# A planner's GpSimd price corrected, and a limit on how far a background step may push attention's scores back

## The chip, the cores and the metric

The kernel runs on one core of a Trainium2 chip. The metric is the time of one execution on the device, in microseconds. The profiled execution is a run of its own with its own time.

## The reference

One conformer block over x of shape (2, 4000, 144), bfloat16, with four heads of 36 and a depthwise convolution of five taps. `_layernorm` has no weights.

```python
h = _layernorm(x); x = x + 0.5 * (_silu(h @ w_ff1a) @ w_ff1b)
h = _layernorm(x); q, k, v = split(h @ w_qkv)          # each (B, H, T, 36)
p = _softmax(q @ k.T * 36 ** -0.5)                      # over 4000 keys
x = x + (p @ v) @ w_o
h = _layernorm(x) @ w_pw1; h = h[..., :144] * _sigmoid(h[..., 144:])
c = sum(pad(h)[:, i:i + T] * dw[i] for i in range(5))   # along time
x = x + _silu(c) @ w_pw2
h = _layernorm(x); x = x + 0.5 * (_silu(h @ w_ff2a) @ w_ff2b)
return _layernorm(x)
```

## The kernel before

**Tiling.** A batch has 4000 tokens in eight chunks: seven of 512 and a last one of 416. Chunks 0 to 7 are batch 0, 8 to 15 batch 1. Within a chunk, a token tile holds 128 tokens (104 in the last chunk), and most steps handle half a chunk, two tiles, at a time (index g).

**Attention.** A group is (batch, query chunk, pair of heads p), 32 groups in all. Within a group an iteration handles 128 keys: `emit_S` issues four score matmuls into two PSUM banks, `emit_exp` one exp on ScalarE over both banks (1024 columns, 832 in the last chunk), `emit_O` four value matmuls into banks 4 and 5. 4000 keys are 31 such iterations and a remainder of 32, which is handled for both pairs together in an iteration of its own in the group with p = 0 (tile PR). Two sets of banks alternate, so the scores of iteration n wait for the exp of n - 2. When the last values of a group are issued, `epilogue` copies banks 4 and 5 out on VectorE (OTA, OTF), transposes OTF on TensorE and divides by the sums (AN). The next group's first values may only be issued when OTF is done.

**Background.** All other work of a chunk is a background step: `ff1` and `pre2` (first feed-forward, then keys, queries and values) ahead of its attention, `post1` (output projection, residual, gate `glu`) and `post2` (convolution `conv`, second feed-forward, last layer norm, store) behind it. The convolution of chunk c waits for `glu` of chunk c + 1, unless c is its batch's last. During attention, gates use tanh on ScalarE (tile TH), which shares its function table with exp, and only banks 6 and 7 are open to background steps. Two series of `post2` run beside each other, for even and odd chunks.

**Layer norm.** `ln` takes statistics on VectorE (`bn_stats`, `bn_aggr`), adds epsilon and raises to -0.5 on GpSimd (tile RS), and normalises two tiles (XN). In the middle of attention (`rest`) the normalise is always on GpSimd. Before all keys of batch 0 are there, and after the last exp, it takes GpSimd or VectorE, by a comparison of planned times. `transp` then transposes XN on TensorE.

**The order.** All engines run their queues in order, and a planner in Python writes the order out. `Rec.op` keeps a planned time for each engine: an instruction starts when its engine is free and its operands are done, lasts `cost`, and is done `LAT` later; on TensorE a change of `kind` adds 0.13. Every background step is a generator (`Thread`) that yields the engine it needs next. `Sched.best` takes, among the threads in list order, the first whose start lies within 0.15 of the earliest. The main loop compares that start t with a, the time at which the next scores can start:

```python
a = s_start(n_s) if n_s < NIT else R.free["pe"]
t, th = S.best()
if th is not None and (a is None or t < a or (th.req[0] == "act" and t < a + 0.05)):
    S.run(th)
```

So a background step goes ahead of the next scores if it starts before them, however long it is. `a` is None while the keys of the next scores' chunk are not there. The planned costs of TensorE steps are 0.24 for a half's transposes or projection, 0.43 for a feed-forward, gate or projection tile, 0.60 for the ten matmuls of a feed-forward's second product, 0.84 for the epilogue's transposes and 1.07 for one half of a convolution.

Every instruction is recorded through one line, so the profile gives all of them line L135; tiles tell them apart.

Of the kernel before, what the change touches and what calls it, by code (L numbers as in the profile page):

```python
# [145 lines left out]
class Slots:  # L146
# [11 lines left out]
    def best(self):  # L158
        return min(self.free.values())
# [11 lines left out]
class Thread:  # L171
    def __init__(self, gen, ready):
        self.gen, self.ready, self.live = gen, ready, True
        self.req = ("none", None, (), None)


def need(eng, slots=None, kids=(), cond=None):
    return (eng, slots, kids, cond)


class Sched:
# [38 lines left out]
            th.ready = max(th.ready, max(o.done for o in new))  # L220

    def start_of(self, th):
        eng, slots, kids, cond = th.req
        if any(k.live for k in kids) or (cond is not None and not cond()):
            return None
        t = max([th.ready] + [k.ready for k in kids])
        if slots is not None:
            if not slots.free:
                return None
            t = max(t, slots.best())  # L230
        return max(t, self.R.free[eng]) if eng in self.R.free else t

    def best(self, window=0.15):
        c = [(self.start_of(th), th) for th in self.threads]
        c = [(t, th) for t, th in c if t is not None]
        if not c:
            return None, None
        lim = min(t for t, _ in c) + window
        return next((t, th) for t, th in c if t <= lim)

    def run(self, th):
        eng, slots, kids, cond = th.req
        for k in kids:
            th.ready = max(th.ready, k.ready)
        self.advance(th, slots.take() if slots is not None else None)


def bass_standalone__conformer_family_zipformer__speech_kernel(
# [31 lines left out]
    R = Rec(nc)  # L280
    op = R.op
    S = Sched(R)
# [4 lines left out]
    NXN, NXT, NTH, NHT, NSW = 8, 6, 6, 3, 2  # L287
    NPT = 6
    NU = 5
    NWARM = 36  # L290
    X = sb("X", [NBLK, D])
    XN = sb("XN", [NXN, 2, D])
    ST = sb("ST", [NXN, 2, 6], F32)
    MV = sb("MV", [NXN, 2, 2], F32)
# [4 lines left out]
    HT = sb("HT", [NHT, 9, CH // 2])  # L299
# [108 lines left out]
    banks = Slots(R, range(8))  # L408
# [14 lines left out]
            op("dve", "tensor_copy", dst, src, r=r, w=w, cost=dve)  # L423

    def setup_dw():
        bk = yield need("pe", banks)
        for k in range(2):
            op("pe", "transpose", PSH[0:HD, bk, k * 8:k * 8 + KCONV], DWR[0:KCONV, k * HD:(k + 1) * HD],
               IDENT[0:KCONV, 0:KCONV], r=["DWR", "ID"], w=[("ps", bk)], kind="s")
        yield need("dve")  # L430
        op("dve", "tensor_scalar", DWT[0:HD, :, 0:KCONV],
           PSH[0:HD, bk, 0:16].rearrange("p (k n) -> p k n", k=2)[:, :, 0:KCONV], 0.5, None, op0=ALU.mult,
           r=[("ps", bk)], w=["DWT"])
        banks.give(bk)
# [13 lines left out]
    def transp(c, src, rk, s, g):  # L448

        n = tb(c)  # L450
        bk = yield need("pe", banks)
        dst = PSH[0:HD, bk, 0:512].rearrange("p (k i n) -> p k i n", k=2, i=2)
        for k in range(2):
            for i in range(2):
                op("pe", "transpose", dst[:, k, i, 0:n], src[:, i, k * HD:(k + 1) * HD], IDENT[0:n, 0:n],
                   r=rk + ["ID"], w=[("ps", bk)], cost=0.06, kind="f")
        yield need("dve")
        xd = XT[0:HD, s, :, g * 2 * n:(g + 1) * 2 * n].rearrange("p k (i n) -> p k i n", i=2)
        copy(xd, dst[:, :, :, 0:n], [("ps", bk)], [("XT", s, g)], 0.37, 0.48)
        banks.give(bk)  # L460

    def ln(c, g):
        n = tb(c)
        u = yield need("dve", xnp)
        for i in range(2):
            op("dve", "bn_stats", ST[0:n, u, i, :], X[0:n, c * NB + 2 * g + i, :], r=[("X", c, 2 * g + i)],
               w=[("ST", u, i)], cost=0.233)
        yield need("dve")
        for i in range(2):
            op("dve", "bn_aggr", MV[0:n, u, i, :], ST[0:n, u, i, :], r=[("ST", u, i)], w=[("MV", u)], cost=0.09)  # L470
        op("pool", "tensor_scalar", RS[0:n, u, :, 1], MV[0:n, u, :, 1], LN_EPS, None, op0=ALU.add,
           r=[("MV", u)], w=[("VE", u)], cost=0.25)
        op("pool", "tensor_tensor", RS[0:n, u, :, 0], RS[0:n, u, :, 1], NHALF[0:n, :], op=ALU.pow,
           r=[("VE", u), "NHALF"], w=[("RS", u)], cost=0.6)
        rest = not (mode["front"] or mode["tail"])
        yield need("pool" if rest else "dve")
        for i in range(2):
            ready = R.last
            e = "dve"
            if rest or max(R.free["pool"], ready) + 0.5 < max(R.free["dve"], ready) + 0.25:  # L480
                e = "pool"
            op(e, "tensor_scalar", XN[0:n, u, i, :], X[0:n, c * NB + 2 * g + i, :], MV[0:n, u, i, 0:1],
               RS[0:n, u, i, 0:1], op0=ALU.subtract, op1=ALU.mult, r=[("X", c, 2 * g + i), ("MV", u), ("RS", u)],
               w=[("XN", u, i)], cost=0.25 if e == "dve" else 0.56)
        return u

    def ln_tr(c, s, g):
# [1 line left out]
        yield from transp(c, XN[0:tb(c), u, :, :], [("XN", u, 0), ("XN", u, 1)], s, g)  # L489
        xnp.give(u)  # L490

    def residual(c, g, mm, scale, rk, cost=0.06):

        bk = yield need("pe", banks)
        for i in (2 * g, 2 * g + 1):
            terms = mm(i)
            for t, (l, rh) in enumerate(terms):
                op("pe", "matmul", PSV[0:tb(c), bk, (i % 2) * D:(i % 2 + 1) * D], lhsT=l, rhs=rh, start=t == 0,
                   stop=t == len(terms) - 1, r=rk, w=[("ps", bk)], cost=cost, kind="f")
        yield need("dve")  # L500
        op("dve", "scalar_tensor_tensor", out=xv(c, g), in0=PSV[0:tb(c), bk, 0:2 * D].rearrange("p (i d) -> p i d", i=2),
           scalar=scale, in1=xv(c, g), op0=ALU.mult, op1=ALU.add, r=[("ps", bk)] + xk(c, g), w=xk(c, g), cost=0.46)
        banks.give(bk)
# [20 lines left out]

    def ff_tile(c, s, h, m, WA, nm, silu):

        bk = yield need("pe", banks)
        n = nc_(c)
        wk = [(nm, "a", j) for j in range(4)]
        if m < 4:  # L530
# [20 lines left out]
    def ff(c, s, WA, WB, nm, silu, then):  # L551

        h = yield need("pe", htp)
        n = tb(c)
        kids = S.spawn(ff_tile(c, s, h, m, WA, nm, silu) for m in range(5))
        yield need("pe", kids=kids)
        xtp.give(s)

        def half(g):
            yield from residual(  # L560
                c, g,
                lambda i: [(ht(h, m, CH)[:, i * n:(i + 1) * n], WB[:, m, :]) for m in range(4)]
                + [(ht(h, 4, CH // 2)[:, i % 2 * n:(i % 2 + 1) * n], WB[:, 4 + i // 2, :])],
                0.5 if silu else 0.25, [("HT", h)] + [(nm, "b", j) for j in range(5)])
            yield from then(g)

        kids = S.spawn(half(g) for g in range(2))
        yield need("pe", kids=kids)
        htp.give(h)

    def proj(Tt, Wt, nm, c, s, p):
        n = nc_(c)
        bk = yield need("pe", banks)
        for k in range(2):
            op("pe", "matmul", PSV[:, bk, 0:n], lhsT=Wt[0:HD, k, 2 * p:2 * p + 2, :].rearrange("p h d -> p (h d)"),
               rhs=XT[0:HD, s, k, 0:n], start=k == 0, stop=k == 1, r=[("XT", s, 0), ("XT", s, 1), nm], w=[("ps", bk)],
# [5 lines left out]
    def vproj(c, s, g):  # L582

        tiles = [j for j in (2 * g, 2 * g + 1) if (j + 1) * KTL <= nc_(c)]
        bk = yield need("pe", banks)
        for j in tiles:
            for k in range(2):
                op("pe", "matmul", PSV[:, bk, (j % 2) * D:(j % 2 + 1) * D], lhsT=XT[0:HD, s, k, j * KTL:(j + 1) * KTL],
# [9 lines left out]
    def vrem(c, s):  # L598

        b = c // CPB  # L600
        r0 = nc_(c) - REM
        bk = yield need("pe", banks)
        for h in range(H):
            for k in range(2):
                op("pe", "matmul", PSV[32 * h:32 * h + 32, bk, 0:DH], lhsT=XT[0:HD, s, k, r0:r0 + REM],
# [47 lines left out]

    def glu(c, s, hf):
        cc = c % CPB
        bk = yield need("pe", banks)
        n, nt = nc_(c), tb(c)
        mm2(c, WP1, s, D + hf * HD, D + (hf + 1) * HD, bk, HD, ["WP1"])
        t = yield from tanh(n, bk, HD)
        banks.give(bk)  # L660
        bk = yield need("pe", banks)
        mm2(c, WP1, s, hf * HD, (hf + 1) * HD, bk, HD, ["WP1"])
        yield need("dve")
        op("dve", "scalar_tensor_tensor", out=U[0:HD, c % NU, hf, :, 1:1 + nt],
# [37 lines left out]

    def conv(c, z, hf, silu):
        v, n, nt = c % NU, nc_(c), tb(c)
        bk = yield need("pe", banks)
        o = PSV[0:HD, bk, 0:n].rearrange("p (i n) -> p i n", i=NB)
        u = U[0:HD, c % NU, hf, :, :]
        parts = [(2, 0, 4, 0, 1), (1, 1, 4, 0, 1), (1, 0, 1, 3, 0), (0, 2, 4, 0, 1), (0, 0, 2, 2, 0),
# [52 lines left out]
    def epilogue(b, qc, p, gi):  # L761
# [2 lines left out]
        op("dve", "tensor_copy", OTA[:, 0:n], PSV[:, 4, 0:n], r=[("ps", 4)], w=["OTA"], cost=0.63)  # L764
        op("dve", "tensor_tensor", OTF[:, gi % 2, 0:n], PSV[:, 5, 0:n], OTA[:, 0:n], op=ALU.add,
           r=[("ps", 5), "OTA"], w=[("OTF", gi % 2)], cost=0.63)
        bk = yield need("pe", banks)
        for i in range(NB):
            op("pe", "transpose", PSV[0:nt, bk, i * 128:(i + 1) * 128], OTF[:, gi % 2, i * nt:(i + 1) * nt],
               IDF[:, :], r=[("OTF", gi % 2), "IDF"], w=[("ps", bk)], cost=0.21, kind="f")  # L770
        if p == 0:
            an_of[c] = yield need("dve", anp)
        a = an_of[c]
        yield need("dve")
        v = PSV[0:nt, bk, :].rearrange("p (i h d) -> p i h d", i=NB, h=2)
        op("dve", "reciprocal", RD[0:nt, gi % 2, :, :], v[:, :, :, DH], r=[("ps", bk)], w=[("RD", gi % 2)],
           cost=0.14)
# [108 lines left out]

    while n_e < NIT:
        a = s_start(n_s) if n_s < NIT else R.free["pe"]
        t, th = S.best()
        if th is not None and (a is None or t < a or (th.req[0] == "act" and t < a + 0.05)):  # L890
            S.run(th)
            if mode["front"] and len(kv_done) == CPB:
# [56 lines left out]
```

## Time and profile before

| | us |
|---|---|
| median of 3 runs | 1149.72 (1145.28 to 1159.77) |
| profiled execution | 1162.85 |
| its span, first to last instruction | 1161.0 |
| ScalarE busy | 1043.6 (90%) |
| TensorE busy | 963.1 (83%), granted clock 0.962 of full on average |
| VectorE, GpSimd busy | 467.4 (40%), 354.3 (31%) |

The profile is of one execution, and its time stands above the runs of the table's first line. In the rows, PE is TensorE, PEld its weight loads, ACT ScalarE, DVE VectorE and POOL GpSimd. A bracket at a row's end is the idle time of that engine just before it, with what ended it.

### The profile page before, as it was taken

How to read it: one execution, taken by the hardware profiler on the slowest of the kernel's cores; microseconds unless marked ns; L12 is line 12 of the kernel's file. 1: busy time of each engine (PE TensorE's matmuls, PEld its weight loads, DVE VectorE, ACT ScalarE, POOL GpSimd, SP SyncE). 2: the span in 40 equal slices, each digit the busy share in tenths (PEclk: the TensorE clock that was granted, in tenths of full speed). 3: DMA queues.
4: the chain of work that ended last, by engine and by line, in shares of the span. 5: the costliest groups of instructions: out<-in, count | busy, mean ns of one | idle time of the engine just before them, and what ended most of it. 6: DMA issues, size and time to landing. Idle time of an engine off the chain costs nothing.

```text
span 1161.0 us, 25201 instructions
## 1 busy us (share of the span) xinstructions
PE 963.1 (83%) x10834; PEld 368.7 (32%) x10834; DVE 467.4 (40%) x1445; ACT 1043.6 (90%) x1274; POOL 354.3 (31%) x595
## 2 busy tenths in 40 slices
PE   8998887999989887787879887787878787887966
PEld 4633232333333332232323221232322232222324
DVE  6875443565555543241332430241323232242424
ACT  3789999999999999999997999999999999999952
POOL 3421423354545433122232330122213123132122
PEclk8999999999999999999996899999999999999976
DMA  4000000000000000000000000000000000000000
GB/s 114 2 1 1 2 1 1 1 2 5 4 7 1 1 7 6 1 1 6 2 7 1 6 5 1 1 1 6 2 6 1 6 1 6 1 4 5 1 6 10
DMA packets 9496, 7.22 MB, mean 6 GB/s; under 512 B 2808, under 2 KB 9384, under 8 KB 9384
## 3 DMA queue, kind: packets, MB, share of 16 engines
q1 hardware_dynamic: 8228, 5.13, 1.5%
q8 instruction: 85, 1.39, 0.5%
q10 hardware_dynamic: 1156, 0.47, 0.2%
q14 instruction: 27, 0.22, 0.1%
HBM read 3.30 MB, written 2.30 MB: 5 GB/s over the span
## 4 chain that ended last, share of the span: by engine, by line
ACT 40%; PE 33%; POOL 16%; DVE 7%; issue 2%; DMA 0%; ACTq 0%; POOLq 0%; DVEq 0%
ACT PT L135 35%; PE PS L135 33%; POOL XN L135 9%; POOL RS L135 6%; ACT TH L135 5%; DVE ST L135 2%; DVE X L135 1%; DVE HT L135 1%; DVE MV L135 1%; DVE XN L135 1%; DVE SW L135 0%; DMA WQKV<-in_w_qkv_dram 0%; DVE VA L135 0%; DVE OTF L135 0%; DVE QT L135 0%
## 5 line engine op out<-in xcount | busy, mean ns | idle before, releaser
L135 ACT ACTIVATE PT<-PS 128x1024 bf16<-128x1024 f32 (+1 forms) x992 | 925.4, 1051 | 31.7 <-PE PS L135 28.8
L135 PE MATMUL PS<-QT,KT 64*64 64x512 bf16 (+1 forms) x3968 | 405.1, 398 | 116.9 <-ACT PT L135 112.8
L135 PE MATMUL PS<-PT,VA 64*64 64x512 bf16 (+1 forms) x3968 | 381.4, 378 | 0.6 <-ACT PT L135 0.6
L135 POOL TENSOR_SCALAR RS<-MV 128x2 f32<-128x2 f32 (+1 forms) x160 | 36.5, 228 | 705.0 <-DVE MV L135 704.9
L135 PEld LDWEIGHTS PS<-QT,KT 64*64 64x64 bf16 x3968 | 113.0, 104 | 433.1 <-ACT PT L135 363.3
L135 POOL TENSOR_SCALAR XN<-X,MV,RS 128x144 bf16<-128x144 bf16 (+1 forms) x236 | 199.6, 856 | 9.3
L135 PEld LDWEIGHTS PS<-PT,VA 64*64 64x64 bf16 x3968 | 116.5, 107 | 17.2 <-issue 8.8
L135 POOL TENSOR_TENSOR RS<-RS,NHALF 128x2 f32<-128x2 f32 (+1 forms) x160 | 114.7, 717 | 13.3
L135 DVE COPY XT<-PS 72x512 bf16<-72x512 bf16 (+1 forms) x144 | 57.8, 411 | 145.0 <-PE PS L135 144.5
L135 DVE COPY OTA<-PS 128x512 f32<-128x512 f32 (+1 forms) x32 | 21.7, 679 | 226.1 <-PE PS L135 226.0
L135 ACT ACTIVATE TH<-PS 128x512 bf16<-128x512 f32 (+5 forms) x170 | 99.5, 585 | 14.4 <-PE PS L135 13.2
L135 PE MATMUL PS<-XT,WA 72*128 72x512 bf16 (+3 forms) x384 | 93.5, 365 | 9.5 <-DVE HT L135 8.6
L135 DVE SCALAR_TENSOR_TENSOR HT<-TH,PS 128x512 bf16<-128x512 bf16 (+3 forms) x110 | 67.8, 624 | 75.1 <-ACT TH L135 75.1
L135 PE MATMUL PS<-IDENT,XN 128*72 128x128 bf16 (+1 forms) x512 | 51.1, 228 | 45.8 <-POOL XN L135 35.7
L135 DVE SCALAR_TENSOR_TENSOR X<-PS,X 128x288 bf16<-128x288 f32 (+1 forms) x128 | 57.6, 451 | 64.3 <-PE PS L135 63.3
L135 DVE BATCH_NORM_STATS2 ST<-X 128x6 f32<-128x144 bf16 (+1 forms) x320 | 81.6, 297 | 3.3
L135 PEld LDWEIGHTS PS<-IDENT,XN 128*72 128x72 bf16 (+1 forms) x512 | 33.8, 116 | 91.8 <-POOL XN L135 69.1
L135 PE MATMUL PS<-WB,HT 128*128 128x144 bf16 (+1 forms) x640 | 52.9, 236 | 2.5 <-DVE HT L135 0.7
L135 PEld LDWEIGHTS PS<-XT,WA 72*128 72x128 bf16 x384 | 31.2, 103 | 64.5 <-DVE HT L135 23.3
L135 PEld LDWEIGHTS PS<-WB,HT 128*128 128x128 bf16 (+1 forms) x640 | 43.3, 107 | 22.5 <-DVE HT L135 10.6
L135 PE MATMUL PS<-U,DG 72*72 72x256 bf16 (+7 forms) x288 | 46.9, 317 | 1.8 <-POOL U L135 1.5
L135 DVE BATCH_NORM_AGGREGATE MV<-ST 128x2 f32<-128x6 f32 (+1 forms) x320 | 45.4, 170 | 0.0
(66 smaller groups left out, 519.0 us busy)
## 6 DMA issues: line engine op xcount, KB each, us to landing
X<-in_x_dram SPq DMA_DIRECT2D x14, 144.0 KB, 3.2
out_dram<-XN SPq DMA_DIRECT2D x28, 72.0 KB, 1.6
X<-in_x_dram SPq DMA_DIRECT2D x2, 117.0 KB
out_dram<-XN SPq DMA_DIRECT2D x4, 58.5 KB
WA<-in_w_ff1a_dram ACTq DMA_DIRECT2D x1, 144.0 KB
WB<-in_w_ff1b_dram ACTq DMA_DIRECT2D x1, 144.0 KB
WA<-in_w_ff2a_dram SPq DMA_DIRECT2D x1, 144.0 KB
WB<-in_w_ff2b_dram SPq DMA_DIRECT2D x1, 144.0 KB
```

Source lines behind the costliest of these rows:

```text
L135: ins = getattr(eng, o.name)(*o.a, **o.k)
```

## The change

The planner's cost of a normalise on GpSimd goes from 0.56 to 0.86, also in the comparison that chooses its engine, and that of an aggregate on VectorE from 0.09 to 0.12. Each request for TensorE now carries the step's planned duration (`dur`). `Sched.best` gets a limit, the start of the next scores plus SLACK = 0.7, and leaves out the TensorE steps whose start, duration and 0.13 (0.26 if a score or value step, kind "q", is the last on TensorE) would end behind it. Without a next start (`a` is None), and in the loops before attention and after its last values, there is no limit. In `epilogue`, a pair with p = 1 waits until its chunk has its AN slot.

```diff
-def need(eng, slots=None, kids=(), cond=None):
-    return (eng, slots, kids, cond)
+def need(eng, slots=None, kids=(), cond=None, dur=0.0):
+    return (eng, slots, kids, cond, dur)
...
-    def best(self, window=0.15):
+    def best(self, window=0.15, before=None):
+
         c = [(self.start_of(th), th) for th in self.threads]
         c = [(t, th) for t, th in c if t is not None]
+        if before is not None:
+            extra = 0.26 if self.R.kind == "q" else 0.13
+            c = [(t, th) for t, th in c if not th.req[4] or t + th.req[4] + extra <= before]
         if not c:
             return None, None
...
+    SLACK = 0.7
...
     def transp(c, src, rk, s, g):
-        bk = yield need("pe", banks)
+        bk = yield need("pe", banks, dur=0.24)
...
-            op("dve", "bn_aggr", MV[0:n, u, i, :], ST[0:n, u, i, :], r=[("ST", u, i)], w=[("MV", u)], cost=0.09)
+            op("dve", "bn_aggr", MV[0:n, u, i, :], ST[0:n, u, i, :], r=[("ST", u, i)], w=[("MV", u)], cost=0.12)
...
-            if rest or max(R.free["pool"], ready) + 0.5 < max(R.free["dve"], ready) + 0.25:
+            if rest or max(R.free["pool"], ready) + 0.86 < max(R.free["dve"], ready) + 0.25:
...
-               w=[("XN", u, i)], cost=0.25 if e == "dve" else 0.56)
+               w=[("XN", u, i)], cost=0.25 if e == "dve" else 0.86)
...
     def ff_tile(c, s, h, m, WA, nm, silu):
-        bk = yield need("pe", banks)
+        bk = yield need("pe", banks, dur=0.43)
...
     def conv(c, z, hf, silu):
-        bk = yield need("pe", banks)
+        bk = yield need("pe", banks, dur=1.07)
...
     def epilogue(b, qc, p, gi):
-        bk = yield need("pe", banks)
+        bk = yield need("pe", banks, dur=0.84)
...
         if p == 0:
             an_of[c] = yield need("dve", anp)
+        yield need("dve", cond=lambda: c in an_of)
         a = an_of[c]
-        yield need("dve")
...
-        t, th = S.best()
+        t, th = S.best(before=None if a is None else a + SLACK)
```

The other requests for TensorE get their durations in the same way: 0.1 in `setup_dw`, 0.24 in `residual`, `vproj` and `vrem`, 0.60 in the `residual` of a feed-forward, 0.43 in `proj` and in both of `glu`.

## Rows read from the trace of the kernel before

**Rows 1.** The page: busy time of the engines, then tenths in 40 slices.

```profile
PE 963.1 (83%) x10834; PEld 368.7 (32%) x10834; DVE 467.4 (40%) x1445; ACT 1043.6 (90%) x1274; POOL 354.3 (31%) x595
...
ACT  3789999999999999999997999999999999999952
...
PEclk8999999999999999999996899999999999999976
```

**Rows 2.** The list of waits: us in total, times, longest us.

```profile
PEld PS L135 <- POOL XN L135: 69.1, 70, 2.1
...
ACT PT L135 <- PE PS L135: 28.8, 68, 1.3
```

**Rows 3.** Timeline of PE, chunk 10's attention: start us, us, what [idle before].

```profile
748.76 0.41 PE L135 MATMUL PS<-IDENT,XN 128*72 128x128 bf16 x4 [1.00 <-POOL XN L135]
...
767.37 0.41 PE L135 MATMUL PS<-IDENT,XN 128*72 128x128 bf16 x4 [1.19 <-POOL XN L135]
```

**Rows 4.** Timeline of ACT, the same stretch.

```profile
749.57 1.02 ACT L135 ACTIVATE PT<-PS 128x1024 bf16<-128x1024 f32 x1 [0.65 <-PE PS L135]
...
768.17 0.60 ACT L135 ACTIVATE PR<-PS 128x512 bf16<-128x512 f32 x1 [0.84 <-PE PS L135]
769.03 0.60 ACT L135 ACTIVATE TH<-PS 128x512 bf16<-128x512 f32 x1 [0.27 <-PE PS L135]
769.52 1.93 ACT L135 ACTIVATE PT<-PS 128x1024 bf16<-128x1024 f32 x2
```

**Rows 5.** Timeline of POOL, the same stretch.

```profile
743.07 0.23 POOL L135 TENSOR_SCALAR RS<-MV 128x2 f32<-128x2 f32 x1 [53.81 <-DVE MV L135]
...
745.87 0.23 POOL L135 TENSOR_SCALAR RS<-MV 128x2 f32<-128x2 f32 x1
```

**Rows 6.** Tile XN: ns min/median/max, first and last start us, forms.

```profile
L135 POOL TENSOR_SCALAR XN<-X,MV,RS x236: 852/855/864, 101.5 to 1107.7; 128x144 bf16<-128x144 bf16 x108, 104x144 bf16<-104x144 bf16 x10
L135 DVE TENSOR_SCALAR XN<-X,MV,RS x84: 299/312/319, 10.1 to 1158.6; 128x144 bf16<-128x144 bf16 x64, 104x144 bf16<-104x144 bf16 x20
```

**Rows 7.** Timeline of ACT, batch 0.

```profile
122.77 1.02 ACT L135 ACTIVATE PT<-PS 128x1024 bf16<-128x1024 f32 x1 [0.28 <-PE PS L135]
...
369.85 6.87 ACT L135 ACTIVATE PT<-PS 128x1024 bf16<-128x1024 f32 x7 [0.39 <-PE PS L135]
...
431.64 0.59 ACT L135 ACTIVATE TH<-PS 72x512 bf16<-72x512 f32 x1 [0.80 <-PE PS L135]
```

**Rows 8.** Timeline of PE, a convolution half in batch 1.

```profile
754.89 1.29 PE L135 MATMUL PS<-U,DG 72*72 72x512 bf16 x9
```

**Rows 9.** Timeline of ACT, the last exps.

```profile
1101.92 12.26 ACT L135 ACTIVATE PT<-PS 128x832 bf16<-128x832 f32 x16
```

**Rows 10.** Busy us by windows behind the last exp (columns named in the answer).

```profile
core 0: us, PE busy (x) PEld busy (x) DVE busy (x) ACT busy (x) POOL busy (x), PEclk, DMA share, GB/s
...
1115.00:1120.00 5.00, 2.75 (x20) 2.08 (x20) 2.48 (x7) 0.51 (x1) 0.00 (x0) 0.70 0.00 0
1120.00:1125.00 5.00, 1.12 (x8) 0.73 (x8) 2.68 (x13) 0.75 (x2) 2.03 (x5) 0.50 0.01 3
1125.00:1130.00 5.00, 3.66 (x10) 1.68 (x11) 1.17 (x2) 2.59 (x4) 0.23 (x2) 0.50 0.00 0
```

**Rows 11.** Windows of 1 us where the clock falls.

```profile
607.00:608.00 1.00, 0.06 (x4) 0.00 (x0) 0.00 (x0) 1.00 (x2) 1.00 (x3) 1.00 0.00 0
...
609.00:610.00 1.00, 1.00 (x7) 0.19 (x2) 0.00 (x0) 0.95 (x1) 0.00 (x0) 0.50 0.00 0
```

**Rows 12.** Windows of 10 us around the falls.

```profile
610.00:620.00 10.00, 10.00 (x60) 3.18 (x63) 1.17 (x2) 6.17 (x9) 0.23 (x2) 0.50 0.01 2
620.00:630.00 10.00, 10.00 (x70) 4.25 (x66) 1.94 (x4) 6.55 (x9) 0.00 (x0) 0.50 0.00 0
...
640.00:650.00 10.00, 8.74 (x106) 3.94 (x106) 5.83 (x15) 9.77 (x13) 0.42 (x2) 1.00 0.01 2
...
660.00:670.00 10.00, 10.00 (x72) 3.29 (x68) 2.79 (x6) 8.19 (x11) 0.00 (x0) 0.51 0.00 0
```

**Rows 13.** Window of bare attention.

```profile
700.00:720.00 20.00, 14.54 (x184) 4.02 (x180) 2.05 (x4) 19.95 (x23) 0.00 (x0) 1.00 0.01 2
```

More of the change, by code (lines that the diff above doesn't have):

```diff
@@ L173, in __init__ @@
         self.gen, self.ready, self.live = gen, ready, True
-        self.req = ("none", None, (), None)
-def need(eng, slots=None, kids=(), cond=None):
-    return (eng, slots, kids, cond)
+        self.req = ("none", None, (), None, 0.0)
+def need(eng, slots=None, kids=(), cond=None, dur=0.0):
+    return (eng, slots, kids, cond, dur)
 class Sched:
@@ L222, in start_of @@
     def start_of(self, th):
-        eng, slots, kids, cond = th.req
+        eng, slots, kids, cond, dur = th.req
         if any(k.live for k in kids) or (cond is not None and not cond()):
@@ L241, in run @@
     def run(self, th):
-        eng, slots, kids, cond = th.req
+        eng, slots, kids, cond, dur = th.req
         for k in kids:
@@ L425, in setup_dw @@
     def setup_dw():
-        bk = yield need("pe", banks)
+        bk = yield need("pe", banks, dur=0.1)
         for k in range(2):
@@ L490, in ln_tr, with residual @@
         xnp.give(u)
-    def residual(c, g, mm, scale, rk, cost=0.06):
-        bk = yield need("pe", banks)
+    def residual(c, g, mm, scale, rk, cost=0.06, dur=0.24):
+        bk = yield need("pe", banks, dur=dur)
         for i in (2 * g, 2 * g + 1):
@@ L563, in half @@
                 + [(ht(h, 4, CH // 2)[:, i % 2 * n:(i % 2 + 1) * n], WB[:, 4 + i // 2, :])],
-                0.5 if silu else 0.25, [("HT", h)] + [(nm, "b", j) for j in range(5)])
+                0.5 if silu else 0.25, [("HT", h)] + [(nm, "b", j) for j in range(5)], dur=0.6)
             yield from then(g)
@@ L572, in proj @@
         n = nc_(c)
-        bk = yield need("pe", banks)
+        bk = yield need("pe", banks, dur=0.43)
         for k in range(2):
@@ L584, in vproj @@
         tiles = [j for j in (2 * g, 2 * g + 1) if (j + 1) * KTL <= nc_(c)]
-        bk = yield need("pe", banks)
+        bk = yield need("pe", banks, dur=0.24)
         for j in tiles:
@@ L601, in vrem @@
         r0 = nc_(c) - REM
-        bk = yield need("pe", banks)
+        bk = yield need("pe", banks, dur=0.24)
         for h in range(H):
@@ L655, in glu @@
         cc = c % CPB
-        bk = yield need("pe", banks)
+        bk = yield need("pe", banks, dur=0.43)
         n, nt = nc_(c), tb(c)
@@ L660, in glu @@
         banks.give(bk)
-        bk = yield need("pe", banks)
+        bk = yield need("pe", banks, dur=0.43)
         mm2(c, WP1, s, hf * HD, (hf + 1) * HD, bk, HD, ["WP1"])
@@ L704, in conv @@
         v, n, nt = c % NU, nc_(c), tb(c)
-        bk = yield need("pe", banks)
+        bk = yield need("pe", banks, dur=1.07)
         o = PSV[0:HD, bk, 0:n].rearrange("p (i n) -> p i n", i=NB)
@@ L766, in epilogue @@
            r=[("ps", 5), "OTA"], w=[("OTF", gi % 2)], cost=0.63)
-        bk = yield need("pe", banks)
+        bk = yield need("pe", banks, dur=0.84)
         for i in range(NB):
```

## The prediction

> **What bounds the kernel now.** The page comes first: ScalarE is busy for 90% of the span, and for 90% or more of every slice from the fourth to the thirty-eighth but one [rows 1]. Between 85 and 1090 us the exps set the pace; TensorE has room beside them. So the question is where ScalarE still idles there. The list of waits names two figures that belong together: TensorE's weight loads waited 69.1 us in 70 cases for a normalised tile (XN) from GpSimd, and exps waited 28.8 us for TensorE [rows 2]. The timeline of one chunk of batch 1 shows how the first makes the second. TensorE executes its queue in order; the transposes of XN at 748.76 and 767.37 sat at the head of that queue for 1.00 and 1.19 us, with the next scores behind them [rows 3]. ScalarE then idled 0.65 us before one exp, and 0.84 and 0.27 us at the second place [rows 4]. So a wait costs ScalarE what it exceeds 0.35 us by (1.00 - 0.65, 1.19 - 0.84).
>
> Why the transposes stand too early is read on GpSimd: one layer norm occupies it from 743.07 to 745.87, 2.80 us [rows 5], of which the two normalises are 2 x 0.855 [rows 6]. The planner believes 0.25 + 0.08 + 0.60 + 0.08 + 2 x 0.56 = 2.13.
>
> **The costs (0.56 to 0.86, 0.09 to 0.12).** The new sum on GpSimd is 2.73 us against 2.80 on the chip. With the aggregate's two additional 0.03 us, the planner's time for the first half's XN moves back by 0.66 us and, since the second half queues behind the first on GpSimd, for the second by some 1.3 us. No instruction gets slower; the transposes move back in TensorE's order, behind scores that don't need them. A transpose moves by whole places, about one exp (1.93 us for two, minus their overlap: some 0.92 [rows 4]) apart. The second halves move at least one place; 1.19 - 0.92 = 0.27 us is under the free 0.35. First halves move a place in about 0.66 / 0.92 = 7 of 10 cases.
>
> What is there to gain: seven chunks have the 0.65 us idle (4.6 us), seven the 0.84 + 0.27 (7.8); two chunks of 416 columns have 0.54 + 0.43 (1.9); the change of batches has 0.83, 1.25 and 0.53 (2.6); twelve idles behind XN waits from 122.77 to 369.85, of which the first and last are the first two of [rows 7], make 4.7. In all 21.6 us. By the two movements some 18 of it are of second halves and go, and 7 tenths of the other 3.6; 2 to 3 us I leave for waits that arise elsewhere, because the order of every engine is planned anew. **Term 1: -18 us**, bounds 0 (nothing moves past a score) and -21.6.
>
> The third place of the same cost is the choice between GpSimd and VectorE, 0.5 to 0.86. It acts only before attention has all its keys and after its end. All 236 normalises of GpSimd lie between 101.5 and 1107.7, and VectorE does the rest [rows 6]: the old figure never chose GpSimd there, so a higher one changes nothing. 0. The new 0.12 also shifts the plan of the front, where no row shows a wait that rests on it: 0, bounds -2 and +2. The new condition on the divisor step (an_of) and the added durations issue no instruction, no DMA and no wait of their own; SP's queue stays as it is.
>
> **The slack.** In planner time a 512-query exp is 0.05 + 1024 x 0.000833 = 0.903, scores and values 0.214 each; TensorE is free 0.903 - 0.428 = 0.475 us ahead of the next scores. A step behind a score or value step passes if its duration + 0.26 is at most the gap + 0.7. Steps of 0.24 and 0.43 always pass; 0.60 needs a gap of 0.16; the epilogue's transposes (0.84) need 0.40; a convolution half (1.07) needs 0.63. So only convolutions are held back in an ordinary gap, and with 416 queries (exp 0.743, gap 0.315) the epilogue's transposes too. A tanh between exps adds 0.477 to the gap, and behind the end of a group the first values wait for OTF, so that it is 0.475 + 0.214 = 0.689: both let a convolution pass.
>
> What the hold gains is small: a convolution is 1.29 us of TensorE [rows 8], but no idle of 0.15 us or more follows this one on ScalarE; the largest behind a convolution at full clock is 0.80 us (the last of [rows 7]), and the 32 together have about 3 us. **Term 2: -1 us**, bounds 0 and -3.
>
> What it costs is lateness. A convolution half becomes ready just behind the tanhs of the next chunk's gate, when bare exps follow, and there may be a wait of half a chunk, some 32 us, for a gap. In the middle of attention this is hidden by stretches with no background step at all. At the end it is not: chunk 13's convolution would have to run in chunk 15, whose gaps are 0.315 and 0.529 without a tanh, so I expect it and its feed-forward behind the last exp. From TensorE's rows of one such chunk (first of twelve in [rows 8]: two convolutions 2.58, residual 0.84, transposes 0.82, feed-forward 2.86 + 1.60) this is 8.7 us at full clock, 17.4 (estimate) at half. Leaving attention it gives ScalarE back 6 x 0.48 + 0.27 = 3.2 us (a tanh delays the next exp by 0.49, 769.03 to 769.52 [rows 4]). After the last exp, which ends at 1101.92 + 12.26 = 1114.18 [rows 9], TensorE is busy 7.53 of 15 us while the last chunk goes through its chain of small steps [rows 10], so some 7.5 us is free, though at a low clock. The last chunk's own chain doesn't get longer; only the thread of odd chunks must finish 13 before 15. **Term 3: +3 us**, near the covered end; bounds -3.2 (wholly covered) and 17.4 - 3.2 = +14.2.
>
> **The clock.** TensorE's granted clock is 1.00 nearly throughout, but falls to 0.50 (the 1.2 GHz level) four times during attention, each time within 2 us of a long XN wait: at 607 to 608 TensorE is busy 0.06 us, at 609 the clock is 0.50 [rows 11]. Then ScalarE does 6.17, 6.55 and 8.19 us of work in 10 where a quiet window has 9.77 [rows 12]: 3.60 + 3.22 + 1.58 = 8.4 us lost. The two short falls and an edge add four idles of 0.94 to 1.30 us, so that it is 12.7. If the waits go, most falls lose what came before them. **Term 4: -9 us of the profiled execution**, bounds 0 and -12.7.
>
> **The sum.** The profiled execution took 1162.85 us, its span 1161.0 and 1.85 around it: 1162.85 - 18 - 1 + 3 - 9 = 1138. It lies 13.1 us over the median of 1149.72, which is about what the falls cost; I take it that a median run loses little to them, so that term 4 is mostly in the median already: 1149.72 - 18 - 1 + 3 = 1134. I forecast 1135 us.
>
> **The rivals.**
> B, both go wholly: all 21.6 us of waits, convolutions free, the late chunk covered (-3.2), and a median run that still had 4 us of falls to lose: 1149.7 - 21.6 - 3 - 3.2 - 4 = 1118, with a little left over 1121. For it: the same rows return chunk by chunk, so one good order repeats. Against it: a plan fixed in one place tends to shift a wait.
>
> C, the change doesn't do what it says: the new cost is right for GpSimd, but the plan still has exps at 0.903 us against some 0.92 and matmul steps shorter than recorded ones; transposes land in the same places or other waits come up. Term 1 is then 0 to -5: 1149.7 - 3 + 3 = 1150.
>
> D, the slower side: convolutions starve. Bare batch-1 attention offers a sure gap only at the end of a group, two per chunk, and there the epilogue's transposes come first in one of them; with one half per chunk served, two needed, post-attention work piles up behind the last exp. At the half clock of the present tail each chunk costs 17.4 - 3.2 = 14.2 us: three give 1149.7 - 19 + 43 = 1174. It is slower than before from the second chunk on (28 against 19). Against it: as soon as one pair is through, its feed-forward's five tanhs open gaps for the other thread, so the pile should stop at one or two.
>
> E, the clock speaks against the change: held steps leave longer bare stretches with less TensorE work, and the clock falls there. Two more falls of the price above (some 8 us each) give 1135 + 16 = 1151. Against it: the bare stretch from 700 to 720 us has TensorE busy 14.54 of 20 and a clock of 1.00 [rows 13]. The Trainium skill, TensorE: Matmul & The Clock Gate, section HAM oscillation, says that gaps in TensorE's work send the clock back to its lower level until activity releases it. By that rule E could happen wherever a gap is left, and the four falls behind XN waits agree with it; a bare stretch alone, at 1.00 here, does not show it.
>
> **How the numbers follow.** Forecast 0.50 (1126 to 1144), B 0.20, C 0.14, D 0.11, E 0.05. The range of 1117 to 1163 leaves out the best of B and the upper part of D, less than 2 in 10. Two per cent of the median is 23 us, about what can be told from no change: under 1126.7 lie B and the lower edge of the forecast, 0.24; above 1172.7 half of D, 0.06; the rest, 0.70, within.
>
> **What would show it.** In the profile after, the wait of weight loads for GpSimd's XN should fall from 69.1 to under 20 us, the 0.65 and 0.84 us idles ahead of exps should be gone in batch 1, the chunk's period should shrink by 1 to 2 us, and clock falls between 100 and 1090 us should be fewer. Convolutions should stand beside tanhs or ends of groups; the last before the final exp tells the size of term 3: if several pairs follow the last exp and the tail grows past 55 us (47 now), D holds. The prediction is wrong if XN waits stay (C), if ScalarE's idle moves to other releasers, or if the tail grows more than attention shrinks.

## The result, and the profile after

The changed kernel took 1120.29 us (median of 4 runs, 1120.03 to 1121.79), the kernel before 1150.62 beside it (1145.28 to 1159.77): a ratio of 0.9731, 95% interval 0.9668 to 0.9794. That is 30 us faster where 15 were forecast. The time lies inside the range and almost on rival B's 1121, but not by B's account, as the stages show. One of e2's four runs below (1168.78 us, clock 0.83) fell in the chip's slower state and is left out.

The page of the kernel after, its busy line and tenths [rows 1]:

```profile
PE 959.0 (86%) x10834; PEld 365.8 (33%) x10834; DVE 463.5 (41%) x1442; ACT 1035.9 (93%) x1280; POOL 346.9 (31%) x587
...
ACT  3698999999999999999999999999999999999832
...
PEclk8999999999999999999999899999999999999955
```

The list of waits of the same kernel [rows 2]:

```profile
PEld PS L135 <- POOL XN L135: 22.9, 40, 1.2
...
ACT PT L135 <- PE PS L135: 5.0, 15, 0.9
...
PE PS L135 <- POOL XN L135: 4.0, 14, 0.8
```

The last row is TensorE's own idle behind XN, its matmuls' and not its weight loads'. In the list before it was

```profile
PE PS L135 <- POOL XN L135: 35.7, 52, 1.6
```

ScalarE is now at nine tenths or more in every slice from the fifth to the thirty-seventh; in exchange one slice more is thin at the end, at half clock. The wait for XN has fallen from 69.1 to 22.9 us, that of exps for TensorE from 28.8 to 5.0. The weight loads' waits alone would mislead: 40 are left, but TensorE itself waits 4.0 us for XN where it waited 35.7, and ScalarE next to nothing.

The span falls into four stages: up to the first exp, attention of batch 0 (to the end of its last exp of 832 columns), of batch 1 (to the end of the last exp), and the tail behind. Worked out from such rows of ScalarE's timeline in each profiled execution, in us:

| | front | batch 0 | batch 1 | tail | span |
|---|---|---|---|---|---|
| before | 56.4 | 538.8 | 518.9 | 46.8 | 1161.0 |
| after | 56.2 | 514.5 | 487.1 | 60.5 | 1118.3 |

Attention lost 56.2 us and the tail grew by 13.7: 42.7 us of the profiled execution before, which stands 12.2 over its median. What attention lost is mostly idle time of ScalarE. The window from the first exp to the end of the last, of the kernel before (columns as in rows 10: width, then busy us and instructions of PE, PEld, DVE, ACT, POOL, then the clock):

```profile
56.41:1114.18 1057.77, 881.34 (x10252) 316.01 (x10252) 404.75 (x1169) 1000.99 (x1194) 323.29 (x520) 0.98 0.01 3
```

and of the kernel after:

```profile
56.23:1057.83 1001.60, 865.70 (x10194) 305.87 (x10192) 394.87 (x1145) 987.52 (x1190) 312.52 (x505) 0.99 0.01 3
```

ScalarE was idle for 56.8 of 1057.8 us (1057.77 - 1000.99), now for 14.1 of 1001.6. Its busy time fell as well, from 1001.0 to 987.5. Of these 13.5 us some 3.2 (the prediction's estimate) are seven tanhs of chunk 13, which no longer stand in attention (161 tanhs there against 168). For the rest, a busy time is not a fixed amount of work, because an exp overlaps the one before it (two take 1.92 us together in the timeline below), and one behind an idle takes 1.02 alone [rows 4].

How a chunk looks now, first on TensorE (timeline of the kernel after, batch 1):

```profile
896.63 0.41 PE L135 MATMUL PS<-IDENT,XN 128*72 128x128 bf16 x4 [0.22 <-POOL XN L135]
...
899.44 0.41 PE L135 MATMUL PS<-IDENT,XN 128*72 128x128 bf16 x4 [0.28 <-POOL XN L135]
...
920.80 1.29 PE L135 MATMUL PS<-U,DG 72*72 72x512 bf16 x9
...
923.01 1.29 PE L135 MATMUL PS<-U,DG 72*72 72x512 bf16 x9
```

and on ScalarE, around the two convolutions:

```profile
919.13 3.01 ACT L135 ACTIVATE PT<-PS 128x1024 bf16<-128x1024 f32 x3
922.13 0.59 ACT L135 ACTIVATE TH<-PS 72x512 bf16<-72x512 f32 x1
922.62 1.92 ACT L135 ACTIVATE PT<-PS 128x1024 bf16<-128x1024 f32 x2
924.43 0.60 ACT L135 ACTIVATE TH<-PS 72x512 bf16<-72x512 f32 x1
924.91 11.05 ACT L135 ACTIVATE PT<-PS 128x1024 bf16<-128x1024 f32 x12
```

The transposes of [rows 3], which waited 1.00 and 1.19 us, wait 0.22 and 0.28, under the 0.35 that were free there, and the idles of [rows 4] are gone. Both convolution halves go beside a tanh with no idle on ScalarE. From one chunk's convolution to the next is 61.72 us (859.08 to 920.80); before it was 64.78 (819.60 to 884.38).

The tail, on TensorE's timeline of the kernel after: the transposes of OTF for chunk 14, the last gate of chunk 14, then the convolutions of chunks 13, 14 and 15. The last exp ended at 1057.83.

```profile
1033.60 0.65 PE L135 MATMUL PS<-IDF,OTF 128*128 128x128 f32 x4
...
1051.11 0.62 PE L135 MATMUL PS<-XT,WP 72*72 72x512 bf16 x2
...
1058.18 2.40 PE L135 MATMUL PS<-U,DG 72*72 72x512 bf16 x18
...
1076.06 4.47 PE L135 MATMUL PS<-U,DG 72*72 72x512 bf16 x18
...
1095.64 2.93 PE L135 MATMUL PS<-U,DG 72*72 72x416 bf16 x18
```

Chunk 13's convolution stands behind the last exp, as forecast, and that of chunk 15 starts 37.8 us behind it; before the change 22.1 (1136.30 against 1114.18).

Of the signs that the prediction named, the idles of 0.65 and 0.84 us are gone, convolutions stand beside tanhs, and attention shrank by more than the tail grew. The wait of weight loads for XN was to fall under 20 us and fell to 22.9; the chunk's period was to shrink by 1 to 2 us and shrank by 3.06. The tail passed 55 us, but one chunk's convolution more, not several, follows the last exp.

### The profile page after: what moved, and what is told of

The parts are those of the page before. It is cut to its first block, busy times and chain, and to the rows that moved or that the text cites. A ratio compares the mean times of both kernels' runs of the same rounds, so it can differ in the third digit from the quotient of the medians.

```text
span 1118.3 us, 25219 instructions
## 1 busy us (share of the span) xinstructions
PE 959.0 (86%) x10834; PEld 365.8 (33%) x10834; DVE 463.5 (41%) x1442; ACT 1035.9 (93%) x1280; POOL 346.9 (31%) x587
## 4 chain that ended last, share of the span: by engine, by line
ACT 73%; PE 20%; POOL 3%; DVE 2%; issue 1%; DMA 0%; ACTq 0%; POOLq 0%; DVEq 0%
ACT PT L135 65%; PE PS L135 20%; ACT TH L135 6%; POOL RS L135 2%; POOL XN L135 1%; DVE XN L135 1%; DVE ST L135 0%; DMA WQKV<-in_w_qkv_dram 0%; ACT KT L135 0%; DVE X L135 0%; DVE MV L135 0%; ACT HT L135 0%; ACT XT L135 0%; ACTq L135 0%; DVE VA L135 0%
## 5 line engine op out<-in xcount | busy, mean ns | idle before, releaser
L135 POOL TENSOR_SCALAR XN<-X,MV,RS 128x144 bf16<-128x144 bf16 (+1 forms) x228 | 192.7, 856 | 7.2
L135 PE MATMUL PS<-XT,WA 72*128 72x512 bf16 (+3 forms) x384 | 98.4, 377 | 12.0 <-DVE HT L135 10.4
L135 DVE COPY XT<-PS 72x512 bf16<-72x512 bf16 (+1 forms) x140 | 56.1, 412 | 126.1 <-PE PS L135 125.1
L135 ACT ACTIVATE TH<-PS 128x512 bf16<-128x512 f32 (+5 forms) x165 | 103.0, 624 | 5.7 <-PE PS L135 5.4
L135 DVE SCALAR_TENSOR_TENSOR HT<-TH,PS 128x512 bf16<-128x512 bf16 (+3 forms) x105 | 65.2, 624 | 82.0 <-ACT TH L135 82.0
L135 PEld LDWEIGHTS PS<-IDENT,XN 128*72 128x72 bf16 (+1 forms) x512 | 34.1, 116 | 61.8 <-POOL XN L135 22.9
L135 DVE SCALAR_TENSOR_TENSOR U<-TH,PS 72x512 bf16<-72x512 bf16 (+1 forms) x32 | 21.5, 673 | 54.4 <-PE PS L135 45.2
```

Of the source, the lines that this page charges most:

```text
L135: ins = getattr(eng, o.name)(*o.a, **o.k)
```

## The experiments

The theory: the costs take the XN waits off ScalarE's path, the limit takes the waits behind long steps off it, and the price of the limit is a later end. The rivals: that one of the two parts does all of it; that held convolutions cost more than they give; that the tail is long for another reason. Stages in the same order as above are given for each (front, batch 0, batch 1, tail).

**e1, the costs alone.**

```diff
-        t, th = S.best(before=None if a is None else a + SLACK)
+        t, th = S.best()
```

> The changed kernel with its new costs, but without the limit on background steps (the planner is given no limit). Theory P (the GpSimd price brings the gain, the limit only costs a longer tail): the wait of weight loads for XN falls to some 20 us as in the changed kernel, the tail behind the last exp stays at 47 us, and the time is at or under the changed kernel's, 1108 to 1122 us. Theory S (the limit brings at least half of the gain): the tail is 47 us, but attention keeps small idles behind convolutions and other long steps, and the time is 1128 to 1142 us.

Measured 1120.79 us (1118.52 to 1121.31), ratio 0.9703 (0.9643 to 0.9763); stages 57.0, 521.3, 494.3, 46.6. ScalarE's timeline over one chunk's period of 63.11 us, the rows that have an idle:

```profile
849.97 0.59 ACT L135 ACTIVATE TH<-PS 72x512 bf16<-72x512 f32 x1 [0.45 <-PE PS L135]
...
866.61 0.60 ACT L135 ACTIVATE TH<-PS 128x512 bf16<-128x512 f32 x1 [0.21 <-PE PS L135]
...
875.61 4.69 ACT L135 ACTIVATE PT<-PS 128x1024 bf16<-128x1024 f32 x5 [0.24 <-PE PS L135]
...
896.07 4.69 ACT L135 ACTIVATE PT<-PS 128x1024 bf16<-128x1024 f32 x5 [0.19 <-PE PS L135]
```

The idles of 0.65, 0.84 and 0.27 us are gone; the small rest is not behind XN but behind longer steps, the first of them a convolution. The window over its attention (columns as above):

```profile
56.96:1072.51 1015.55, 866.23 (x10260) 311.61 (x10258) 405.61 (x1174) 993.51 (x1197) 322.27 (x521) 1.00 0.01 3
```

The costs alone give as much as the whole change: their attention is 14.0 us longer (1015.6 against 1001.6), their tail 13.9 shorter. So the limit gives and takes the same amount. Time and tail are those of theory P, but P's account, that the limit only costs, does not hold.

**e2, the limit alone** (the costs 0.56, 0.5 and 0.09 back).

> The changed kernel with the limit, but with the old costs (0.56, 0.09 and 0.5). Theory P: XN waits stay near 69 us, the tail is 60 us, and the time is 1150 to 1165 us. Theory S: XN waits stay near 69 us, but idles behind convolutions go, and the time is 1128 to 1145 us.

Measured 1142.03 us (median of three runs, 1141.72 to 1143.2), ratio 0.9895 (0.9835 to 0.9956); stages 55.8, 524.2, 500.1, 60.1. ScalarE's timeline, one chunk:

```profile
853.74 1.02 ACT L135 ACTIVATE PT<-PS 128x1024 bf16<-128x1024 f32 x1 [0.82 <-PE PS L135]
...
888.46 1.02 ACT L135 ACTIVATE PT<-PS 128x1024 bf16<-128x1024 f32 x1 [0.83 <-PE PS L135]
```

These two, behind XN, are the only idles listed over a chunk's period: the limit cannot see them, since a transpose's planned duration is 0.24 whatever it will wait for. And the long tail is here without the costs. Each part removes its own kind of idle, and the tail is the limit's. The waits of weight loads for XN are 62.0 us, a little under the 69 that both theories expected; the tail is P's and the time S's, so neither theory holds alone here either.

**e3, convolutions free of the limit; e8, the transposes of OTF free of it; e4, no limit in the last two groups.**

```diff
# e3
-        bk = yield need("pe", banks, dur=1.07)
+        bk = yield need("pe", banks)
# e8
-        bk = yield need("pe", banks, dur=0.84)
+        bk = yield need("pe", banks)
# e4
-        t, th = S.best(before=None if a is None else a + SLACK)
+        t, th = S.best(before=None if a is None or its[min(n_s, NIT - 1)][0] >= len(groups) - 2 else a + SLACK)
```

> The changed kernel, with no duration given for the convolution, so that the limit doesn't hold it back and holds only the epilogue's transposes and the feed-forward's second product. If holding the convolutions is what the limit is worth, the time lies some 5 to 10 us over the changed kernel's 1120 us and ScalarE's idle behind convolutions is back; if it is worth 1 us, as predicted, the time is 1112 to 1123 us, depending on whether chunk 13's convolution still lands behind the last exp.

> The changed kernel, with no duration given for the epilogue's transposes. In chunk 15 they then pass as before, and the chain of chunk 14 isn't held up by them; the convolutions stay held, and chunk 13's pair still stands behind the last exp. If the tail's 13.7 us come from the convolution held alone, as predicted, the tail stays at 58 to 61 us and the time at 1118 to 1124 us; if they come from chunk 14's chain being late, the tail falls to 47 to 52 us and the time to 1108 to 1114 us.

> The changed kernel without the limit in the last chunk's two groups (416 queries, where the gap in planner time is 0.315 and the epilogue's transposes and convolutions find none). The second convolution pair that stands behind the last exp goes back ahead of it. If the tail's growth from 47 to 60 us is that chunk's, the tail is 47 to 50 us again, attention is 3 to 4 us longer, and the time is 1108 to 1114 us. If the tail is bound by the last chunk's own chain at half clock whatever stands beside it, the time stays at 1117 to 1123 us.

| | us | ratio (interval) | stages |
|---|---|---|---|
| e3 | 1125.3 | 0.9747 (0.9692 to 0.9803) | 56.4, 521.2, 487.5, 60.8 |
| e8 | 1117.03 | 0.9662 (0.9605 to 0.9719) | 56.1, 512.2, 487.8, 60.9 |
| e4 | 1108.55 | 0.9604 (0.9555 to 0.9654) | 54.8, 515.1, 490.3, 46.2 |

e3's time is the one expected if holding convolutions is worth 5 to 10 us, not 1; e8's tail is the one expected if the convolution alone makes it, its time 1 us under that range; e4 has the shorter of its two times. e4 keeps nearly all of the shorter attention (its 168 tanhs are all in attention again, some 3.2 of the 3.8 us by which it is longer) and has the old tail. Why freeing either step alone does not shorten the tail is seen on TensorE's timelines: the transposes of OTF for chunk 14, its last gate and chunk 13's convolution, which needs that gate. In e4:

```profile
1008.30 0.65 PE L135 MATMUL PS<-IDF,OTF 128*128 128x128 f32 x4 [0.28 <-DVE OTF L135]
...
1024.09 0.62 PE L135 MATMUL PS<-XT,WP 72*72 72x512 bf16 x2
...
1025.82 1.29 PE L135 MATMUL PS<-U,DG 72*72 72x512 bf16 x9 [0.42 <-POOL U L135]
```

In e8:

```profile
1007.86 1.11 PE L135 MATMUL PS<-IDF,OTF 128*128 128x128 f32 x4 [0.28 <-DVE OTF L135]
...
1025.06 0.62 PE L135 MATMUL PS<-XT,WP 72*72 72x512 bf16 x2
...
1056.47 2.40 PE L135 MATMUL PS<-U,DG 72*72 72x512 bf16 x18
```

In e3:

```profile
1038.88 0.66 PE L135 MATMUL PS<-IDF,OTF 128*128 128x128 f32 x4
...
1056.39 0.62 PE L135 MATMUL PS<-XT,WP 72*72 72x512 bf16 x2
...
1058.12 1.29 PE L135 MATMUL PS<-U,DG 72*72 72x512 bf16 x9 [0.42 <-POOL U L135]
```

Two holds stand in a row, and each suffices; e4 lifts both, with every other hold in the last two groups. With the convolution free (e3) the transposes of OTF still wait for the next group's end, and the gate, which the convolution needs, comes late. With these free (e8) the gate is early, but the convolution is held for 31 us, to the last exp. In the kernel after it is the transposes that are late, by 25 us against e4 (1033.60 against 1008.30), and the convolution is then held for the 6 us that are left until the last exp ends.

**e6, no limit in chunks 7 and 15; e7, e4 with SLACK = 1.0; e5, e4 with a normalise priced at 1.16 instead of 0.86.**

```diff
# e6, against the changed kernel
+        t, th = S.best(before=None if a is None or groups[its[min(n_s, NIT - 1)][0]][1] == CPB - 1 else a + SLACK)
# e7, against e4
-    SLACK = 0.7
+    SLACK = 1.0
# e5, against e4
-               w=[("XN", u, i)], cost=0.25 if e == "dve" else 0.86)
+               w=[("XN", u, i)], cost=0.25 if e == "dve" else 1.16)
```

> The changed kernel without the limit in both chunks of 416 queries, chunk 7 and chunk 15. Chunk 7 is in the middle, and the work held there is done in the next chunk beside exps. If lateness costs only where nothing comes after it, freeing chunk 7 brings no gain, and the time is 1107 to 1112 us, like that of the kernel with only the last chunk free. If held work costs in the middle too, the time is under 1106 us.

> The kernel without the limit in the last chunk, with the limit at 1.0 us in place of 0.7. A convolution now passes in a gap of 0.33 us, so in an ordinary one, and 0.60 and 0.84 always pass: what is left of the limit is little. If the limit's worth in attention (10 us between the run with the costs alone and the one without the limit in the last chunk) comes from holding these steps, the time goes back to that of the costs alone, 1117 to 1122 us; if it came from the mere reordering, it stays at 1107 to 1113 us.

> The kernel without the limit in the last chunk, with the GpSimd normalise priced at 1.16 us in place of 0.86 (0.856 measured). If the price works by keeping the transposes behind scores that don't need them, a price that is too high does the same: XN waits fall from 22.9 us to under 10, and the time is within 4 us of the 1108.6 us of its twin. If the order needs the right price, layer norms planned 0.6 us late per pair cost places elsewhere and the time is 1113 to 1125 us.

| | us | ratio (interval) | stages |
|---|---|---|---|
| e6 | 1109.05 | 0.9596 (0.9548 to 0.9644) | 56.4, 518.3, 485.9, 46.9 |
| e7 | 1117.44 | 0.9675 (0.9628 to 0.9723) | 55.3, 518.9, 494.6, 46.9 |
| e5 | 1105.74 | 0.9569 (0.9523 to 0.9616) | 56.1, 511.4, 488.2, 48.2 |

e6 equals e4: the place where the limit harms is the last chunk, and lifting it at the end of batch 0 too does nothing more. e7 shows that the figure 0.7 decides: with 0.3 us more, attention is 8.0 us longer than in e4 (1013.4 against 1005.4), four fifths of the way back to no limit at all (1015.6 in e1). In e5, the list of waits has

```profile
PEld PS L135 <- POOL XN L135: 1.6, 3, 0.8
```

so some 21 us of the weight loads' XN waits went (22.9 us in e4, as in the kernel after), and the time fell by 3 us at most, where the intervals of e4 and e5 overlap. TensorE's own idle behind XN was 4.2 us in e4 and is nothing in e5: what was left of the waits was worth next to nothing to ScalarE. e5 has the lowest median here.

**e9, chunk 15's steps in a thread of their own** (the changed kernel otherwise; the order up to the last exp is as after the change).

```diff
-                    S.add(series(post2(c) for c in range(par, NCH, 2)))
+                    S.add(series(post2(c) for c in range(par, NCH - 1, 2)))
+                S.add(post2(NCH - 1))
```

> The changed kernel, with chunk 15's post-attention steps in a thread of their own instead of behind chunk 13's in the series of odd chunks. The order up to the last exp stays as in the changed kernel; chunk 13's convolution still comes behind the last exp. Serial theory: the longer tail (60.5 us against 46.8 before) is not chunk 13's work itself but that chunk 15 had to wait for it in the same series, so the tail falls to 47 to 52 us and the time from 1120 to 1107 to 1114. Rival, work theory: TensorE at half its clock has too much to do there, whatever the order; then the tail stays at 58 to 61 us and the time at 1117 to 1122.

Measured 1112.27 us (1111.32 to 1113.47), ratio 0.9655 (0.9636 to 0.9675); stages 54.7, 515.1, 484.9, 54.7. The time is in the serial theory's range, the tail between the two. TensorE's timeline, the convolutions of chunks 14 and 15 behind a last exp that ended at 1054.77:

```profile
1072.73 4.47 PE L135 MATMUL PS<-U,DG 72*72 72x512 bf16 x18
...
1079.66 1.94 PE L135 MATMUL PS<-U,DG 72*72 72x416 bf16 x9
```

and windows of the same stretch:

```profile
1070.00:1075.00 5.00, 5.00 (x18) 2.58 (x16) 0.96 (x2) 2.21 (x4) 0.23 (x2) 0.50 0.02 3
1075.00:1080.00 5.00, 5.00 (x25) 3.39 (x24) 0.54 (x2) 2.17 (x4) 0.00 (x0) 0.50 0.00 0
1080.00:1085.00 5.00, 5.00 (x35) 4.57 (x34) 3.63 (x16) 0.51 (x1) 1.86 (x4) 0.50 0.00 0
```

Chunk 15's convolution starts 24.9 us behind the last exp instead of 37.8, nearly as before (22.1). But from 1070 to 1085 TensorE has no free moment at half its clock, with chunk 13's feed-forward among that work. So of the 13.7 us by which the tail grew, waiting in the same series was 5.9; the other 7.8 stay. The rows put them down to chunk 13's work itself, but no run takes that work alone out of the tail. Neither theory holds alone.

**e10, half the price (0.71) and no limit.**

> The changed kernel without the limit, and with the price of a normalise on GpSimd half way, 0.71 instead of 0.86 (0.56 before; the whole price without the limit gave 1120.8). Theory of whole places: a transpose only moves when the planned time crosses the next scores, so half the price moves the second halves (twice 0.15 and more) but few of the first; waits for XN between 30 and 50 us, time 1127 to 1142. Rival: any rise suffices, since only the part of a wait over 0.35 us reaches ScalarE; then waits under 30 us and a time of 1117 to 1125. A third outcome, waits and time as before the change (above 60 us, above 1142), would say that nothing moves until the full 0.3 is added.

Measured 1130.96 us (1129.15 to 1133.85), ratio 0.9819 (0.9795 to 0.9843), attention 1026.2 us. The list of waits:

```profile
PEld PS L135 <- POOL XN L135: 43.3, 66, 1.2
...
ACT PT L135 <- PE PS L135: 14.9, 51, 1.4
```

Both numbers lie in the ranges of the theory of whole places, but do not single it out: half of e1's effect would be waits of 45 us and a time of some 1135 us, inside the same ranges. Half the price gave 20.5 us (1151.48 beside it to 1130.96) of the 32 that the whole price gave in e1, and took off 26 of 47 us of XN waits (69.1 to 43.3; 21.6 in e1).

**e11, e5 with each exp priced 0.02 us higher** (0.07 instead of 0.05 in its cost).

> The best kernel so far (normalise priced at 1.16, no limit in the last two groups, 1105.7 us) with each exp priced 0.02 us higher in the plan, 0.923 for 512 queries, as the trace has it (0.92). Theory that the exp's price is the same kind of error and still costs: the planned gaps widen by 0.02 and the steps stand nearer to where the chip has them free; attention loses 2 to 6 us of its idle, time 1099 to 1104. Rival: the attention of the best kernel is already bound by ScalarE's own work (under 15 us idle in 1000), and what is left are gaps of another kind; then 1104 to 1109, or worse if the wider planned gap lets more steps pass the limit.

Measured 1106.37 us (1106.2 to 1107.1), ratio 0.9605 (0.9584 to 0.9627), attention 1001.8 us against 999.7 in e5. The rival holds: the exp's price was no error that still cost something.

## Why the prediction was right and wrong

**Term 1, the XN waits (-18): right in its mechanism, too small.** Chunk by chunk the working was close: the seven chunks were to give 12.4 / 7 = 1.77 us each, and the chunk's period in e1 is 64.78 - 63.11 = 1.67 shorter. The costs alone took 32 us off the median, though (1153.0 beside e1 to 1120.8). The idle that the prediction counted is about what went: ScalarE's idle in attention fell by 34.7 us in the profiled executions (56.8 to 22.0, windows above), and 21.6 behind XN waits and 12.7 in clock falls had been counted. The rest is in three places. The sum took 18 of the 21.6. It priced an idle at its own length alone, while ScalarE's busy time fell by 7.5 us beside it (1001.0 to 993.5, with the same exps and tanhs); part of that is the overlap which an exp behind an idle lacks. The list has 119 idles in attention before and 63 in e1, and 56 times 1.02 - 0.92 = 0.10 us would be 5.6 (estimate). And a median run of the kernel before still lost something to falls, which only rival B allowed for: the runs beside e1 lie on about 1 us per 0.001 of mean granted clock (1149.91 at 0.974, 1163.98 at 0.960), and e1's runs had 0.977 to 0.980, so that some 3 to 6 us of the 32 are the clock's (estimate). Together 18 + 3.6 + 7.5 + 3 to 6 make the 32 and a little more.

The free 0.35 us is not a constant. It was read at the two places of [rows 3]; elsewhere in the same trace a wait of 0.69 us left an idle of 0.64:

```profile
183.97 0.41 PE L135 MATMUL PS<-IDENT,XN 128*72 128x128 bf16 x4 [0.69 <-POOL XN L135]
...
184.77 1.02 ACT L135 ACTIVATE PT<-PS 128x1024 bf16<-128x1024 f32 x1 [0.64 <-PE PS L135]
```

**Term 2, the limit's gain (-1): the step that failed.** I looked for idles of 0.15 us and more behind convolutions and found 3 us, and took it that only convolutions would be held. The chunk's period says otherwise: 63.11 in e1, 62.30 in e3, where all but convolutions are under the limit, and 61.72 after. So the other steps give 0.81 us a chunk and the convolutions 0.58. In all, attention is 14.0 us shorter than in e1 (1015.6 to 1001.6); some 3.2 of it is chunk 13's tanhs, which term 3 had, so the limit's own gain is about 10.8, and e4 is 12.2 us of the median under e1. Two things were overlooked. The idles behind the other steps were in the list before, chunk after chunk of batch 1: 0.22 us behind two feed-forward tiles, 0.23 behind a feed-forward's second product, 0.19 behind the transposes of OTF, 0.64 together. e1 keeps them (0.21, 0.24 and 0.19), and in e3 none of them is listed over a chunk.

```profile
775.03 0.60 ACT L135 ACTIVATE TH<-PS 128x512 bf16<-128x512 f32 x1 [0.22 <-PE PS L135]
...
781.22 23.02 ACT L135 ACTIVATE PT<-PS 128x1024 bf16<-128x1024 f32 x25 [0.23 <-PE PS L135]
...
804.42 9.27 ACT L135 ACTIVATE PT<-PS 128x1024 bf16<-128x1024 f32 x10 [0.19 <-PE PS L135]
```

By the working with ordinary gaps these steps pass the limit; which planned gap each met, and so why they were held, was not looked into. And convolutions were priced in the order of the kernel before, where no idle followed the one of [rows 8]; with the new costs alone one half of each pair leaves 0.45 us (849.97 in e1).

**Term 3, the late end (+3): right in its place, at the wrong end of its bounds.** Chunk 13's convolution did land behind the last exp, and the tail grew by 13.7 us; less the 3.2 that its tanhs give back in attention that is 10.5, against an upper bound of 14.2, and lifting the limit there (e4) is worth 11.7. I chose the covered end because TensorE had 7.5 us free there. The sentence that should have been priced stood right beside it: the thread of odd chunks must finish 13 before 15. e9 measures it at 5.9 us; the remaining 4.6 are near the +3. The forecast also named what held it, a convolution with no sure gap and transposes of OTF that don't pass with 416 queries; e3 and e8 show both.

Terms 2 and 3 were to give +2 together and gave about 0 (1120.79 to 1120.29). That the two errors of the limit cancelled is luck; the miss in the sum is all the costs'.

**Term 4, the clock (-9, mostly in the median already): about right.** The profiled execution lost 42.7 us (1162.85 to 1120.15), the median 30.3, so 12.4 of it was the profiled run's own, where the sum had 13.1. Mean granted clocks of runs of the kernel before, taken beside the experiments, say it directly: 1149.91 us at 0.974, 1153.01 at 0.972, 1163.98 at 0.960. The XN waits' falls did go: e1 has none after 105 us. But the kernel after has three others in attention after 105 us, with 13.7 us at 0.50 in all, where the four falls before had 41. Its windows of 2 us show the longest, and TensorE's timeline the row ahead of it:

```profile
634.00:636.00 2.00, 1.52 (x14) 0.37 (x14) 0.69 (x1) 2.00 (x5) 1.81 (x3) 1.00 0.11 35
636.00:638.00 2.00, 1.00 (x16) 0.37 (x12) 1.88 (x3) 2.00 (x4) 0.00 (x0) 0.70 0.12 37
638.00:640.00 2.00, 2.00 (x18) 0.32 (x10) 0.00 (x0) 1.28 (x2) 0.00 (x0) 0.50 0.00 0
640.00:642.00 2.00, 2.00 (x20) 0.79 (x16) 0.76 (x2) 1.54 (x3) 0.00 (x0) 0.50 0.00 0
642.00:644.00 2.00, 2.00 (x20) 0.79 (x12) 0.35 (x1) 1.90 (x2) 0.00 (x0) 0.59 0.00 0
...
637.05 0.64 PE L135 MATMUL PS<-QT,KT 64*64 64x512 bf16 x4 [1.00 <-ACT PT L135]
```

TensorE waits for nothing from GpSimd here. It is the end of a group, where values wait for OTF, and TensorE stood idle for 1.00 us until an exp let the next scores go; the clock drops to 0.50, and ScalarE loses 6 - 1.28 - 1.54 - 1.90 = 1.3 us. So a fall without an XN wait exists, as rival E has it, at a sixth of E's price of 8 us; that held steps cause it was not tested, and e5 and e11, which have the limit too, have no fall between 105 us and their last exp. The rule that E drew on, the Trainium skill, TensorE: Matmul & The Clock Gate, section HAM oscillation, agrees with this row as with those before in that the fall comes with a gap in TensorE's work, though the page speaks of longer gaps than the 1.00 us here. That each fall needs a wait for XN, as I read the rows before, does not hold.

**The threshold and the front (0).** GpSimd's normalises went from 236 to 228 and VectorE's from 84 to 92, all eight in the tail, which has more work there; in e1, with the new threshold and no limit, they are 236 and 84 as before, so the threshold did nothing, as forecast. The front stayed at 56.2 us (56.4).

**The rivals.** B came out in time and not in kind: the late chunk was not covered (+10.5 instead of -3.2), but the limit gave some 10.8 instead of 3. C is refuted by the XN waits and by e1. D's price for one chunk, 14.2 us, compares with 10.5, and its pile stopped at one, as said against it.

## What to carry to other kernels

Price a planner's step by what the trace shows, and a wait by the part of it that reaches the engine that sets the pace: raising one price by 0.30 us was worth 32 us here (with the aggregate's 0.03, which no run takes apart from it), and a further 0.30, which removed 21 us of weight-load waits, at most the 3 us between e4 and e5. A limit on background work needs a place where it ends: what it holds back falls due when the work that it protects runs out, and it should be lifted one chunk earlier (e4, 12 us). Before a limit is called nearly free of effect, add up the idles behind every kind of step that it can hold, not behind the longest alone: 0.64 us a chunk stood in the list before.

## What was not expected of the hardware

TensorE's clock fell to 0.50 for some 6.8 us (1.2 + 4 + 1.6, worked out from the clocks of the windows above) around an idle of 1.00 us. ScalarE's busy time in attention for the same 992 exps and 168 tanhs was 10.2 us less in e4 than before (1001.0 to 990.8), with fewer idles between them. In the tail of e9 the granted clock stayed at 0.50 through the 15 us from 1070 to 1085, in which the rows show TensorE busy throughout.
